# Gate steps placed behind the sums of squares, weight copies each released at its own slot, and a reordered end of attention, in a fused attention and top-capacity MoE kernel

## The chip, the core and the metric

The kernel runs on one core of one Trainium2 chip. The metric is the device time of one execution in microseconds. Before the change it is 424.39 us, the median of 3 runs (422.96 to 424.91).

## What is computed

Attention with RMS-normed q and k (8 batches, 12 heads, 448 tokens, head size 64, all float32), then a mixture of experts on its output (3584 tokens of 768 features, 8 experts, hidden size 1024, at most 80 tokens for each expert).

```
q_n, k_n = rmsnorm(q, g_q), rmsnorm(k, g_k)
attn = softmax(q_n @ k_n.T / sqrt(64))          # the 1e-9 in the sum left aside
x = (attn @ v) as 3584 x 768
logits = x @ w_gate;  expert = argmax(logits);  gate_w = softmax(logits)[expert]
for each expert e:
    tok = tokens of e; if more than 80: the 80 with the largest gate_w
    out[tok] = gate_w[tok] * (relu(x[tok] @ w1[e]) @ w2[e])      # all other rows are 0
```

## The kernel before

**Tiling.** A batch has 12 heads, handled as 3 groups of 4 heads, so there are 24 groups. A group has 7 rows of work: `score` makes a [128, 2, 448] tile of transposed scores (L359) and its exponential (`at`, L362), `av` adds it into `po` (L376), `presum` adds it on VectorE into `sm`, the sums of the softmax (L392, L394).

**Slots.** The order on every engine is written out by hand. The loop at L791 walks over slots; slot s scores rows 2s and 2s+1 and finishes rows 2s-2 and 2s-1, so 3.5 slots are a group, 10.5 a batch and 84 (NS) the whole of attention. Other work hangs on slots in tables: `begins` (ahead of the scores), `pre`, `mid` (behind the presums), `ahead` and `end` (behind `av`). Engines run their own queues in that order, so a step that waits holds up all that stands behind it on its engine.

**Preparing a group.** A group's q and k are loaded by SyncE (L242). ScalarE squares them (L270), VectorE sums the squares (`ms`, L278), ScalarE makes 1/rms from them (`rs`, L289, L290), VectorE refines it (L291 to L293) and scales q and k (`qn`, L306), TensorE transposes (L314), ScalarE copies out of PSUM (`qkT`, L347, L349). The tiles of q and k have four buffers, that is two groups.

**PSUM.** Scores, half of the transposes and the gate's scratch share one tag, `sc`, with two buffers: the next score must wait until ScalarE has emptied the tile two places earlier.

**The gate of a batch** follows 5 to 9 slots behind the start of its third group (b0): `zl` (L411) and `gate1` bring logits and softmax sums together, `gate1v` (L439) divides them, `gate2` (L465) finds maximum and one-hot, `gate2x` takes the exponential and copies the one-hot (L481, L483, ScalarE), `gate2b` the gate's weight `gw` (L489, L491), `gate2p` splits it into bf16 parts on GpSimd (L518 to L521, L512). `merge` then puts the batch's best 80 tokens of each expert into a running list: `row`, `vbeat`, `vtied`, `vahead`, `counts`, `vput`, `place`, `turn`.

**Weights.** The first three experts' weights are fetched straight into SBUF (`fetch_held`, L669), the other five are cast into a bf16 scratch in DRAM by 20 copies from GpSimd's queue (`stage_w`, L201 to L205) and read from there later by SyncE (`fetch_late`).

**The end.** L828 to L935 do the last batch's gate and merge step by step, with filler matmuls (`busy`) that keep TensorE running. Then each expert gathers its rows (L925), transposes them (`xpose`) and runs two matmuls (L973, L992). Weights of the sixth expert (NW0+2) are fetched at L873 and L964, those of the last two when the first two experts are done.

Of the kernel before, what the change touches and what calls it, by code (L numbers as in the profile page):

```python
# [10 lines left out]
F32 = mybir.dt.float32  # L11
# [10 lines left out]
def kernel(  # L22
# [13 lines left out]
    nc = tc.nc  # L36
# [161 lines left out]
    def staged(e, i):  # L198
        return wb_dram[e - NW0, i].rearrange("(c p f) -> p c f", p=128, c=(DC, FC)[i])

    def stage_w(e, i, half):  # L201
        src = (moe_w1, moe_w2)[i][e].rearrange("(c p) f -> p c f", p=128)
        c = src.shape[1] // 2
        nc.gpsimd.dma_start(out=staged(e, i)[:, half * c:half * c + c],
                            in_=src[:, half * c:half * c + c])  # L205
# [27 lines left out]
    with av_stack:  # L233
# [290 lines left out]
        def merge(b):  # L524
# [76 lines left out]
            def vput():  # L601
# [8 lines left out]
                    m["put"][:], iota[:, :].unsqueeze(1).to_broadcast([128, NT, CAP]),  # L610
                    rank[:].unsqueeze(2).to_broadcast([128, NT, CAP]), op=ALU.is_equal)
                m["keep"] = tpool.tile([CAP, E, CAP], BF16, tag="keep", name="keep")
                nc.vector.tensor_tensor(
# [15 lines left out]
            def turn():  # L629
                ps = scratch(BF16)  # L630
                for r in range(2):
# [4 lines left out]
            return [[row, lambda: vbeat((0, 1))], [experts, lambda: vbeat((2, 3)), vtied],  # L636
                    [own, vahead], [counts, vput], [place], [turn]]

# [56 lines left out]
        def at_slot(where, s, f, *a):  # L695
            where.setdefault(s, []).append((f, a))

        ahead = {}

# [17 lines left out]
        for g in range(NG):  # L717
# [3 lines left out]
            if g:  # L721
                for a in range(2):
                    at_slot(mid, b0 - 7 + a if g > 1 else -1, square, g, a)
                    at_slot(end, b0 - 7 + a if g > 1 else -1, squares, g, a)
                at_slot(mid, b0 - 5 if g > 1 else 0, rstd, g)
                for a in range(2):
                    at_slot(mid, b0 - 5 + a if g > 1 else 0, normalise, g, a)
            if g:
# [6 lines left out]
        for b in range(B):  # L735
# [12 lines left out]
            at_slot(end, b0 + 6, gate1t, b)  # L748
            at_slot(mid, b0 + 7, gate1v, b)
            at_slot(mid, b0 + 7, gate2, b)  # L750
            at_slot(mid, b0 + 8, gate2i, b)
            at_slot(end, b0 + 8, gate2x, b)
            at_slot(pre, b0 + 9, gate2b, b)
            at_slot(pre, b0 + 9, gate2p, b)
            for t, fs in enumerate(merge(b)):


                if b == B - 2 and t > 3:
                    at_slot(end, b0 + 12 + t, fs[0])
                    continue  # L760
                s = 15 + b % 2 if b < B - 2 else 13
                (first if t else lambda *a: at_slot(end, *a))(
                    b0 + (10, 10, 12, s, 18 + b % 2, 20 + b % 2)[t], fs[0])
                for n, f in enumerate(fs[1:]):
                    at_slot(end, b0 + (10, 11, 12, s)[t], f)
        at_slot(begins, 0, load_wgs)
# [10 lines left out]
        for e in range(E):  # L777
            for i in range(2):
                s = 9 + 23 * (2 * e + i) // 5
                if e < NW0:  # L780
                    at_slot(mid, s, fetch_held, e, i)
                    continue
                for half in range(2):
                    at_slot(begins, s + 2 * half, stage_w, e, i, half)

# [5 lines left out]
        for s in range(-10, NS + 6):  # L791
# [16 lines left out]
            for r in A2:  # L808
                if r % RD < RD - 1 or r == A2[-1]:
                    av(r)  # L810
            for f, a in ahead.pop(s, []) + end.pop(s, []):
                f(*a)
        assert not ahead
        assert not begins and not pre and not mid and not end
# [36 lines left out]
    for j in range(NT):  # L851
        nc.tensor.matmul(psa[:, 1, j * CAP:(j + 1) * CAP], eqT[:, j * 128:(j + 1) * 128],
                         listT[:3 * E, :], start=True, stop=True)
    busy(4)
    gate2p(b)
    ahead = tpool.tile([128, NT, CAP], BF16, tag="ahead", name="ahead")
    nc.vector.tensor_tensor(
        ahead[:], psa[:, 1, :NT * CAP].rearrange("p (j c) -> p j c", c=CAP),
        gw.unsqueeze(2).to_broadcast([128, NT, CAP]), op=ALU.is_lt)
    R, back = psa[:, 0, :NT * E], psa[:CAP, 1, NT * CAP:NT * CAP + E]  # L860
    for i in range(NT):
# [8 lines left out]
        if i == 0:  # L870

            nc.vector.memset(w_tiles[NW0 + 2][0][0][:, 0, 0:2], 0.0)
            fetch_late(NW0 + 2, (0, ))  # L873
            for j in range(NT):
# [8 lines left out]
                         listn[:CAP, :5])  # L883
    for j in range(NT):
        nc.vector.scalar_tensor_tensor(
            tied[:, j], row[:, j * 128:(j + 1) * 128], gw[:, j:j + 1], tri[:, :],
            op0=ALU.is_equal, op1=ALU.mult)
    for j in range(NT):
# [10 lines left out]
                            rank[:].unsqueeze(2).to_broadcast([128, NT, CAP]), op=ALU.is_equal)  # L899
    psc = scps.tile([128, 2, 512], F32, tag="sc", name="psc")  # L900

    moves = [(identb[:CAP, :CAP], left)] + [(put[:, j, :], m["info"][:, j]) for j in range(NT)]
# [38 lines left out]
    def xpose(e):  # L941
        xg = xgs[e]
        xn = mpool.tile([CAP, DM], BF16, tag="xn", name="xn")
        for i in range(NQ):
# [4 lines left out]
                xg[:, DM + 4 * i:DM + 4 * i + 4].rearrange("p (u hh) -> p u hh", hh=2)  # L949
                .unsqueeze(3).to_broadcast([CAP, 2, 2, D]))  # L950
        pxt = mps.tile([128, DC, CAP], BF16, tag="pxt", name="pxt", bufs=1)
        for c in range(DC):
# [9 lines left out]

    nc.vector.memset(w_tiles[NW0 + 2][1][0][:, 0, 0:2], 0.0)
    fetch_late(NW0 + 2, (1, ))  # L964
    busy(2)
# [78 lines left out]
```

## Time and profile before

| | us |
|---|---|
| median of 3 runs | 424.39 |
| profiled execution | 423.0 |
| its span in the trace | 421.3 |
| attention, first score to the last `po` matmul | 15.6 to 356.1 |
| last gate and gather, until the first expert matmul | 356.1 to 377.3 |
| eight experts | 377.3 to 415 |

TensorE is busy for 399.1 us of the span, VectorE for 357.5, ScalarE for 314.9, GpSimd for 73.5. Attention is 340 us of it, and there all three large engines have little air; the end is a chain of short steps on one engine after the other. TensorE's granted clock is full throughout, but for the store of the last rows.

### The profile page before, as it was taken

The page shows a single profiled execution, that of the slowest core. Times are in us where ns is not written, and L with a number is a line of the kernel's source. Part 1 is how long each engine was busy: PE and PEld are TensorE (multiplying, and loading weights), DVE is VectorE, ACT ScalarE, POOL GpSimd, SP SyncE. Part 2 cuts the span into 40 slices and gives each one's busy share as a digit, 9 for nine tenths or more (in the row PEclk, how much of TensorE's full clock was granted, in tenths as well). Part 3 has the DMA queues.
Part 4 walks back from the last instruction along what each step waited for, and adds up shares of the span by engine and source line. Part 5 has one row for each costly group of instructions (what it writes and reads, how often), then busy time and mean ns, then how long its engine had stood idle before and what let it go on. Part 6 is the DMA issues. An engine that isn't in the chain of part 4 may idle for free.

```text
span 421.3 us, 12543 instructions
## 1 busy us (share of the span) xinstructions
PE 399.1 (95%) x5289; PEld 194.9 (46%) x5289; DVE 357.5 (85%) x641; ACT 314.9 (75%) x479; POOL 73.5 (17%) x118
## 2 busy tenths in 40 slices
PE   6799999999989999999899999999999999889993
PEld 6334444444444445444444444443444443448882
DVE  5699889998999999989999999989999779735550
ACT  5898979997889799979798799878997784202120
POOL 2000001301040205100420024001500050134321
PEclk9999999999999999999999999999999999999999
DMA  7355599999959999999799969999799298869981
GB/s 261 123 149 140 152 224 317 282 254 268 287 166 206 326 230 274 242 237 320 234 236 233 338 172 195 232 286 338 170 237 312 59 358 211 270 213 339 342 301 47
DMA packets 75983, 100.91 MB, mean 240 GB/s; under 512 B 8344, under 2 KB 65176, under 8 KB 75928
## 3 DMA queue, kind: packets, MB, share of 16 engines
q1 hardware_dynamic: 59856, 70.53, 52.2%
q0 software_dynamic: 15776, 29.13, 36.1%
q8 instruction: 41, 0.67, 0.6%
q10 hardware_dynamic: 296, 0.46, 0.4%
q14 instruction: 14, 0.11, 0.1%
HBM read 101.11 MB, written 39.89 MB: 335 GB/s over the span
## 4 chain that ended last, share of the span: by engine, by line
PE 69%; DMA 12%; DVE 10%; ACT 5%; issue 2%; SPq 0%; POOLq 0%; DVEq 0%; ACTq 0%
PE ps L359 26%; PE po L376 26%; DMA w_sb<-wb_scratch 5%; PE zl L411 4%; DMA qk<-in_k_dram 4%; PE tp L314 3%; PE xp L314 3%; DVE ms L278 2%; DVE sm L394 2%; DMA xr_scratch<-xb 2%; PE py L992 1%; DVE qn L306 1%; PE ph L973 1%; ACT qkT L349 1%; DMA xg<-xr_scratch,idxG 1%
## 5 line engine op out<-in xcount | busy, mean ns | idle before, releaser
L359 PE MATMUL ps<-qkT 64*64 64x448 f32 x1344 | 147.9, 548 | 7.6 <-ACT qkT L349 3.2
L362 ACT ACTIVATE at<-ps 128x896 f32<-128x896 f32 x168 | 146.4, 931 | 2.5 <-PE ps L359 1.6
L376 PE MATMUL po<-at,vt 64*64 64x448 f32 x1344 | 142.4, 537 | 0.1
L394 DVE TENSOR_TENSOR sm<-sm,at 128x896 f32<-128x896 f32 x120 | 132.0, 1100 | 2.9
L376 PEld LDWEIGHTS po<-at,vt 64*64 64x64 f32 x1344 | 50.0, 133 | 74.9 <-issue 64.3
L359 PEld LDWEIGHTS ps<-qkT 64*64 64x64 f32 x1344 | 43.1, 132 | 73.2 <-issue 23.5
L278 DVE TENSOR_REDUCE ms<-sq 128x14 f32<-128x896 f32 (+1 forms) x50 | 51.9, 1044 | 6.6 <-ACT sq L270 6.4
L306 DVE TENSOR_TENSOR qn<-qk,rs 128x896 f32<-128x896 f32 (+1 forms) x50 | 52.5, 1052 | 1.9
L270 ACT ACTIVATE sq<-qk 128x896 f32<-128x896 f32 (+1 forms) x50 | 46.3, 929 | 2.8 <-DMA qk<-in_q_dram 2.8
L518 POOL CAST pt<-gw 128x4 bf16<-128x4 f32 x8 | 6.9, 866 | 201.9 <-DVE gw L491 201.9
L977 ACT ACTIVATE h_sb<-ph 128x320 bf16<-128x320 f32 x16 | 7.0, 437 | 39.8 <-PE ph L973 39.8
L654 ACT COPY xb<-xp 128x1024 f32<-128x1024 f32 x24 | 24.3, 1011 | 9.7 <-PE xp L314 9.6
L314 PEld LDWEIGHTS tp<-ident,qn 64*128 64x128 f32 x672 | 23.4, 139 | 11.1 <-issue 5.3
L314 PE MATMUL tp<-ident,qn 64*128 64x64 f32 x672 | 26.9, 226 | 0.0
L383 ACT COPY us<-po 128x896 f32<-128x896 f32 (+1 forms) x24 | 21.4, 893 | 6.2 <-PE po L376 6.2
L392 DVE TENSOR_TENSOR sm<-at 128x896 f32<-128x896 f32 x24 | 25.9, 1081 | 0.0
L347 ACT ACTIVATE qkT<-tp,gqk 128x896 f32<-128x896 f32 x23 | 23.5, 1023 | 0.0
L349 ACT COPY qkT<-tp 128x896 f32<-128x896 f32 x24 | 21.9, 913 | 1.3 <-PE tp L314 1.2
L992 PE MATMUL py<-w_sb,h_sb 128*80 128x384 bf16 (+1 forms) x136 | 22.2, 317 | 0.6 <-DMA w_sb<-wb_scratch 0.6
L996 DVE TENSOR_SCALAR yo<-py,gwT 80x384 f32<-80x384 f32 (+1 forms) x16 | 9.5, 600 | 14.9 <-PE py L992 14.7
L411 PE MATMUL zl<-us,wgs 64*32 64x448 f32 x192 | 21.0, 540 | 0.0
L411 PE MATMUL zl<-sm,zsel 64*32 64x448 f32 x192 | 20.5, 540 | 0.0
(170 smaller groups left out, 412.0 us busy)
## 6 DMA issues: line engine op xcount, KB each, us to landing
wb_scratch<-in_moe_w_dram POOLq DMA_DIRECT2D x20, 768.0 KB, 14.9
w_sb<-wb_scratch SPq DMA_DIRECT2D x9, 1536.0 KB, 8.1
vt<-in_v_dram SPq DMA_DIRECT2D x24, 448.0 KB, 6.3
out_dram<-zeros SPq DMA_DIRECT2D x28, 384.0 KB, 8.2
qk<-in_q_dram SPq DMA_DIRECT2D x23, 448.0 KB, 5.0
qk<-in_k_dram SPq DMA_DIRECT2D x23, 448.0 KB, 6.6
xr_scratch<-xb SPq DMA_DIRECT2D x48, 192.0 KB, 10.2
w_sb<-in_moe_w_dram POOLq DMA_DIRECT2D x6, 1536.0 KB, 15.7
```

What stands on the lines that cost most here:

```text
L270: nc.scalar.activation(st[g]["sq%d" % a][:, lo:hi], st[g]["qk"][a][:, lo:hi], AF.Square)
L278: nc.vector.reduce_sum(out=st[g]["ms"][:, a, lo:hi], in_=st[g]["sq%d" % a][:, lo:hi], axis=AX.X)
L306: nc.vector.tensor_mul(qn[:].rearrange("p (x hh) d -> p hh x d", hh=2)[:, h0:h1], qk[:, lo:hi].rearrange("p (hh x) d -> p hh x d", x=NX), ...
L314: nc.tensor.transpose(o, w, one[p, p], tile_position=(p.start, 0))
L349: nc.scalar.copy(T[:], tp[:, :, :S])
L359: nc.tensor.matmul(ps[u * 64:u * 64 + 64, hh, :S], T1[d, u, x * 64:(x + 1) * 64], T0[d, u, :], start=True, stop=True)
L362: nc.scalar.activation(at[:], ps[:, :, :S], AF.Exp)
L376: nc.tensor.matmul(po[u][hh * D:(hh + 1) * D, u, :S], vt[p, hh * NX + x, :], at[p, hh, :], start=(x == 0), stop=(x == RD - 1))
L392: nc.vector.tensor_add(s["sm"][:], s["at0"][:], s["at1"][:])
L394: nc.vector.tensor_add(s["sm"][:], s["sm"][:], s["at%d" % x][:])
L411: nc.tensor.matmul(t[32 * c:32 * c + 32, r, :S], w, x, start=(i == 0), stop=(i == NQ - 1))
L992: nc.tensor.matmul(py[:, :c1 - c0], h_sb[:, fc, :], chunk(e, 1, fc)[:, c0:c1], start=(fc == 0), stop=(fc == FC - 1))
```

## The change

Six things move.

- **Gate on VectorE and ScalarE.** `gate1v` goes from the middle of its slot to the end, `gate2` from the middle of slot b0+7 to the end of b0+8, and `gate2x`, `gate2b` and `gate2p` to the end of b0+9. So the next group's sums of squares stand ahead of them. The first `normalise` of a batch's first group goes behind the slot's end (`after`), and `vtied` one slot later.
- **Copies.** Each of the 20 copies of weights gets a marker: VectorE sets one element at the copy's slot, GpSimd copies it onto itself and then issues the copy, so that GpSimd can't run ahead of VectorE. The slots are evenly spaced, 2.25 apart from slot 31 to 73; the six direct fetches are at slots 4 to 26 (9 to 32 before).
- **One-hots later.** For the batch before the last, `vput` stands behind the last presums and `keep` at the slot's end.
- **Ties.** In the last merge ScalarE makes the differences gw - row in bf16, and one VectorE instruction over 512 elements makes the ties from them; before, four instructions over 128 each compared and masked.
- **`back`** has its own PSUM tile.
- **Late fetches.** The sixth expert's first weights are fetched right behind `gate2p`, its second ones behind the first expert's first scaled piece.

```diff
+    mark = cpool.tile([1, 4 * (E - NW0)], BF16, name="mark")
     def stage_w(e, i, half):
+        n = 4 * (e - NW0) + 2 * i + half
+        nc.vector.memset(mark[:, n:n + 1], 0.0)
+        nc.gpsimd.tensor_copy(mark[:, n:n + 1], mark[:, n:n + 1])
         src = (moe_w1, moe_w2)[i][e].rearrange("(c p) f -> p c f", p=128)
...
-                    [own, vahead], [counts, vput], [place], [turn]]
+                    [own, vahead], [counts, vput, vkeep], [place], [turn]]
...
-                    at_slot(mid, b0 - 5 + a if g > 1 else 0, normalise, g, a)
+                    s = b0 - 5 + a if g > 1 else 0
+                    at_slot(after if not a and g % NQ == 0 and g > NQ else mid, s, normalise, g, a)
...
-            at_slot(mid, b0 + 7, gate1v, b)
-            at_slot(mid, b0 + 7, gate2, b)
-            at_slot(mid, b0 + 8, gate2i, b)
-            at_slot(end, b0 + 8, gate2x, b)
-            at_slot(pre, b0 + 9, gate2b, b)
-            at_slot(pre, b0 + 9, gate2p, b)
+            at_slot(end, b0 + 7, gate1v, b)
+            at_slot(end, b0 + 8, gate2, b)
+            at_slot(end, b0 + 8, gate2i, b)
+            at_slot(end, b0 + 9, gate2x, b)
+            at_slot(end, b0 + 9, gate2b, b)
+            at_slot(end, b0 + 9, gate2p, b)
...
-                    at_slot(end, b0 + (10, 11, 12, s)[t], f)
+                    if b == B - 2 and t == 3:
+                        at_slot((mid, end)[n], NS, f)
+                    else:
+                        at_slot(end, b0 + (10, 11 + n, 12, s)[t], f)
...
-                s = 9 + 23 * (2 * e + i) // 5
+                n = 2 * e + i
                 if e < NW0:
-                    at_slot(mid, s, fetch_held, e, i)
+                    at_slot(mid, 4 + 9 * n // 2, fetch_held, e, i)
                     continue
                 for half in range(2):
-                    at_slot(begins, s + 2 * half, stage_w, e, i, half)
+                    at_slot(mid, 4 + 9 * (2 * n + half) // 4, stage_w, e, i, half)
...
-            for f, a in ahead.pop(s, []) + end.pop(s, []):
+            for f, a in ahead.pop(s, []) + end.pop(s, []) + after.pop(s, []):
...
     gate2p(b)
+    nc.vector.memset(w_tiles[NW0 + 2][0][0][:, 0, 0:2], 0.0)
+    fetch_late(NW0 + 2, (0, ))
...
-    R, back = psa[:, 0, :NT * E], psa[:CAP, 1, NT * CAP:NT * CAP + E]
+    psc = scps.tile([128, 2, 512], F32, tag="sc", name="psc")
+    R, back = psa[:, 0, :NT * E], psc[:CAP, 1, 64:64 + E]
+    for j in range(NT):
+        nc.scalar.activation(tied[:, j], row[:, j * 128:(j + 1) * 128], AF.Identity,
+                             scale=-1.0, bias=gw[:, j:j + 1])
...
-            nc.vector.memset(w_tiles[NW0 + 2][0][0][:, 0, 0:2], 0.0)
-            fetch_late(NW0 + 2, (0, ))
...
-    for j in range(NT):
-        nc.vector.scalar_tensor_tensor(
-            tied[:, j], row[:, j * 128:(j + 1) * 128], gw[:, j:j + 1], tri[:, :],
-            op0=ALU.is_equal, op1=ALU.mult)
+    nc.vector.scalar_tensor_tensor(
+        tied[:], tied[:], 0.0, tri[:, :].unsqueeze(1).to_broadcast([128, NT, 128]),
+        op0=ALU.is_equal, op1=ALU.mult)
...
+            if e == 0 and i == 0:
+                nc.vector.memset(w_tiles[NW0 + 2][1][0][:, 0, 0:2], 0.0)
+                fetch_late(NW0 + 2, (1, ))
```

**Place 1, VectorE at the gate of batch 3** (of 0 to 7; sm are the presums, rz and lx are `gate1v`, lg to eq are `gate2`, ms the sums of squares of a later group), before the change:

```order
L394 TENSOR_TENSOR sm<-sm,at 128x896 x2
L445 RECIPROCAL rz<-zs 128x12x2 x2
L453 TENSOR_TENSOR lx<-zs,rz 128x12x8 x4
L468 TENSOR_REDUCE lg<-lx 128x32
L471 TENSOR_REDUCE lmax<-lg 128x4
L474 TENSOR_TENSOR lex<-lg,lmax 128x32
L476 TENSOR_TENSOR eq<-lg,lmax 128x32
L477 MEMSET eq 64x8
L278 TENSOR_REDUCE ms<-sq 128x14
L392 TENSOR_TENSOR sm<-at 128x896
L278 TENSOR_REDUCE ms<-sq 128x14
L489 TENSOR_REDUCE lsum<-lex 128x4
```

The same place after the change:

```order
L205 MEMSET mark 1x1
L283 TENSOR_REDUCE ms<-sq 128x14
L450 RECIPROCAL rz<-zs 128x12x2 x2
L458 TENSOR_TENSOR lx<-zs,rz 128x12x8 x4
L397 TENSOR_TENSOR sm<-at 128x896
L283 TENSOR_REDUCE ms<-sq 128x14
L473 TENSOR_REDUCE lg<-lx 128x32
L476 TENSOR_REDUCE lmax<-lg 128x4
L479 TENSOR_TENSOR lex<-lg,lmax 128x32
L481 TENSOR_TENSOR eq<-lg,lmax 128x32
L482 MEMSET eq 64x8
L399 TENSOR_TENSOR sm<-sm,at 128x896 x2
```

All of `gate2` stands behind the second ms now, and `gate1v` behind the first; lsum comes after two more presums.

**Place 2, ScalarE at the same point** (at are the exponentials of scores, rs the 1/rms of a later group, qkT the copies of the transposes of the next one, lex and eqb `gate2x`), before the change:

```order
L627 CAST listn<-mp 80x40
L481 ACTIVATE lex<-lex 128x32
L483 CAST eqb<-eq 128x288
L362 ACTIVATE at<-ps 128x896 x2
L289 ACTIVATE rs<-ms,eps 128x28
L290 ACTIVATE rs<-rs 128x28
L349 COPY qkT<-tp 128x896
L347 ACTIVATE qkT<-tp,gqk 128x896
L362 ACTIVATE at<-ps 128x896 x2
```

The same place after the change:

```order
L634 CAST listn<-mp 80x40
L367 ACTIVATE at<-ps 128x896 x2
L294 ACTIVATE rs<-ms,eps 128x28
L295 ACTIVATE rs<-rs 128x28
L354 COPY qkT<-tp 128x896
L352 ACTIVATE qkT<-tp,gqk 128x896
L486 ACTIVATE lex<-lex 128x32
L488 CAST eqb<-eq 128x288
L367 ACTIVATE at<-ps 128x896 x2
```

The two short instructions of `gate2x` moved from ahead of one pair of exponentials to ahead of the next.

**Place 3, VectorE at the end of attention** (rnk to put are `vput`, us is half of the copy of the last `po`, zsb the last batch's `gate1`), before the change:

```order
L603 TENSOR_TENSOR rnk<-back,eq 128x32
L605 TENSOR_REDUCE rank<-rnk 128x4
L606 SCALAR_TENSOR_TENSOR rank<-rank,cnt 128x4
L609 TENSOR_TENSOR put<-iota,rank 128x320
L613 TENSOR_TENSOR keep<-iota,move 80x640
L394 TENSOR_TENSOR sm<-sm,at 128x896 x2
L385 COPY us<-po 128x448
L418 TENSOR_REDUCE zsb<-zl 128x256
```

The same place after the change:

```order
L399 TENSOR_TENSOR sm<-sm,at 128x896 x4
L608 TENSOR_TENSOR rnk<-back,eq 128x32
L610 TENSOR_REDUCE rank<-rnk 128x4
L611 SCALAR_TENSOR_TENSOR rank<-rank,cnt 128x4
L614 TENSOR_TENSOR put<-iota,rank 128x320
L390 COPY us<-po 128x448
L620 TENSOR_TENSOR keep<-iota,move 80x640
L423 TENSOR_REDUCE zsb<-zl 128x256
```

The last presums pass all of `vput` and keep, and us passes keep.

## Rows read from the trace of the kernel before

**Rows 1.** Page, first part: busy us (share of the span) x instructions, by engine

```profile
PE 399.1 (95%) x5289; PEld 194.9 (46%) x5289; DVE 357.5 (85%) x641; ACT 314.9 (75%) x479; POOL 73.5 (17%) x118
```

**Rows 2.** Waits of PE, 20 to 352 us: total us, times, longest us

```profile
PE ps L359 <- ACT qkT L349: 3.2, 3, 1.2
PE ps L359 <- ACT row L543: 1.3, 3, 0.4
```

**Rows 3.** Timeline, 200 to 222 us: start, duration, engine, line, [idle before <-releaser]

```profile
200.56 0.86 DVE L468 TENSOR_REDUCE lg<-lx 128x32 f32<-128x384 f32 x1
...
201.91 0.23 ACT L481 ACTIVATE lex<-lex 128x32 f32<-128x32 f32 x1 [0.97 <-DVE lex L474]
...
202.13 1.09 DVE L278 TENSOR_REDUCE ms<-sq 128x14 f32<-128x896 f32 x1
...
202.13 0.43 ACT L483 CAST eqb<-eq 128x288 bf16<-128x288 f32 x1
...
204.13 1.08 DVE L278 TENSOR_REDUCE ms<-sq 128x14 f32<-128x896 f32 x1
...
205.25 0.32 ACT L289 ACTIVATE rs<-ms,eps 128x28 f32<-128x28 f32 x1 [1.05 <-DVE ms L278]
...
206.67 0.98 PE L359 MATMUL ps<-qkT 64*64 64x448 f32 x8 [1.23 <-ACT qkT L349]
...
211.63 0.98 PE L359 MATMUL ps<-qkT 64*64 64x448 f32 x8 [0.44 <-ACT row L543]
```

**Rows 4.** Timeline, 200 to 222 us: GpSimd, and VectorE beside it

```profile
207.74 0.20 POOL L520 CAST pt<-left 128x4 bf16<-128x4 f32 x1
...
209.29 2.47 DVE L394 TENSOR_TENSOR sm<-sm,at 128x896 f32<-128x896 f32 x2
...
213.67 2.21 DVE L394 TENSOR_TENSOR sm<-sm,at 128x896 f32<-128x896 f32 x2
```

**Rows 5.** The tile qk: who waited (us, times), landing

```profile
  DMA qk<-in_q_dram: 2.8, 3
...
DMA to landing us min/median/max: 3.1/5.3/17.8
```

**Rows 6.** Timeline, 352 to 372 us, the end of attention and the gate

```profile
354.14 0.81 DVE L613 TENSOR_TENSOR keep<-iota,move 80x640 bf16<-80x640 f32 x1
...
354.88 2.21 DVE L394 TENSOR_TENSOR sm<-sm,at 128x896 f32<-128x896 f32 x2
...
357.13 0.13 PEld L411 LDWEIGHTS zl<-sm,zsel 64*32 64x32 f32 x2 [0.29 <-DVE sm L394]
...
357.67 0.10 PEld L411 LDWEIGHTS zl<-us,wgs 64*32 64x32 f32 x1 [0.40 <-DVE us L385]
...
364.20 0.59 ACT L849 COPY row<-psb 128x512 f32<-128x512 f32 x1
```

**Rows 7.** Timeline, 367.5 to 377.4 us, the last merge and the first transpose

```profile
367.19 0.81 PE L822 MATMUL hot<-tri,identb 128*128 128x512 bf16 x3
...
367.37 0.22 DVE L879 TENSOR_SCALAR stay<-psa,rowF 80x8 bf16<-80x8 f32 x1 [0.35 <-PE psa L868]
...
367.72 1.13 DVE L885 SCALAR_TENSOR_TENSOR tied<-row,gw,tri 128x128 bf16<-128x128 f32 x4
...
369.12 0.19 DVE L893 TENSOR_TENSOR place<-psa,eq 128x32 f32<-128x32 f32 x1 [0.27 <-PE psa L891]
...
377.19 0.06 DVE L963 MEMSET w_sb<- 128x1 uint32 x1
```

**Rows 8.** Groups of instructions: busy us, mean ns | idle before

```profile
L559 DVE TENSOR_TENSOR tied<-row,gw 128x512 bf16<-128x512 f32 x7 | 4.8, 687 | 0.0
...
L561 DVE TENSOR_TENSOR tied<-tied,tri 128x512 bf16<-128x512 bf16 x7 | 3.0, 425 | 0.3
```

**Rows 9.** Chain of waits, 350 to 421.3 us: start, us

```profile
389.00 22.25 DMA w_sb<-wb_scratch
```

**Rows 10.** Timeline, 372 to 422 us, the last expert

```profile
411.74 2.61 PEld L992 LDWEIGHTS <-h_sb 128*80 128x80 bf16 x24 [0.75 <-ACT h_sb L977]
```

More of the change, by code (lines that the diff above doesn't have):

```diff
@@ L611, in vput, with vkeep @@
                     rank[:].unsqueeze(2).to_broadcast([128, NT, CAP]), op=ALU.is_equal)
+            def vkeep():
                 m["keep"] = tpool.tile([CAP, E, CAP], BF16, tag="keep", name="keep")
@@ L696, in at_slot @@
             where.setdefault(s, []).append((f, a))
-        ahead = {}
+        ahead, after = {}, {}
         def first(s, f, *a):
@@ L810 @@
                     av(r)
-            for f, a in ahead.pop(s, []) + end.pop(s, []):
+            for f, a in ahead.pop(s, []) + end.pop(s, []) + after.pop(s, []):
                 f(*a)
-        assert not ahead
+        assert not ahead and not after
         assert not begins and not pre and not mid and not end
@@ L899 @@
                             rank[:].unsqueeze(2).to_broadcast([128, NT, CAP]), op=ALU.is_equal)
-    psc = scps.tile([128, 2, 512], F32, tag="sc", name="psc")
     moves = [(identb[:CAP, :CAP], left)] + [(put[:, j, :], m["info"][:, j]) for j in range(NT)]
@@ L961 @@
     xpose(0)
-    nc.vector.memset(w_tiles[NW0 + 2][1][0][:, 0, 0:2], 0.0)
-    fetch_late(NW0 + 2, (1, ))
     busy(2)
```

## The prediction

> **What bounds the kernel now.** I read the busy shares first, then TensorE's waits, then the timeline at the place of those waits, then the chain through the end. TensorE is busy for 95% of the span, VectorE for 85% [rows 1]; in attention both are near full, so only two kinds of time can come back: TensorE's waits, and the chain of short steps after the last score. Between 20 and 352 us TensorE waits for two things only: three times for ScalarE's copy of transposes (3.2 us) and three times for ScalarE's copy of the row of gate weights (1.3 us) [rows 2]. They come in pairs, in batches 1, 3 and 5, so a pair costs 1.23 + 0.44 = 1.67 us [rows 3] and all three 4.5.
>
> How a pair arises is seen in batch 3 [rows 3]. VectorE works through the gate from 199.4 us; gate2 alone takes from 200.56 to 202.13, and only then come the sums of squares, the second of which ends at 204.13 + 1.08 = 205.21. ScalarE's L289 needs them and began at 205.25 after 1.05 us of idling. Behind it in ScalarE's queue stand the copies of the transposes, whose PSUM tile TensorE's next score needs. So VectorE's gate reaches TensorE through ScalarE's order, not directly.
>
> **The gate moved: -2.1 us.** In the new order gate2's 202.13 - 200.56 = 1.57 us stands behind the second sum, which then ends at 203.64, before ScalarE is free at 205.25 - 1.05 = 204.20. The whole 1.05 us of idling goes, and of TensorE's first wait 1.23 - 1.05 = 0.18 is left. But lex and eqb, 0.23 + 0.43 = 0.66 us [rows 3], now stand between the copies and the next exponentials. Before, they lay ahead of an earlier pair, where ScalarE waited 0.97 us for them. From that point on ScalarE is only 1.05 - 0.66 = 0.39 us ahead, and the row copy that ends the second wait is in its queue. So a batch gives back between 0.39 (ScalarE decides to the end) and 1.67 (TensorE does). The wait of 0.44 for the row says that ScalarE ends the stretch, so I stay near the lower end: 0.7 a batch, 2.1 for three, with ends 1.2 and 4.5. In batches 0, 2 and 4 lex and eqb also move ahead of other exponentials. Rows 2 shows no wait of TensorE there, so I cost it at nothing; if that cover is missing it is 3 x 0.66 = 2.0 us lost, and the worst for this part is 2.0 - 1.2 = 0.8 us slower. What is late next is the gate's weight gw, now two presums and a refinement later on VectorE; the row's transposes wait for it, and about nothing remains of its air.
>
> **The copies: 0.** VectorE gets 20 more settings of 0.06 us (as one of the same kind takes, the last row of [rows 7]), 1.2 us in all, and GpSimd 20 copies of one element, 0.2 us each when undisturbed [rows 4]. Behind a waiting marker in GpSimd's queue stand the weight copy and gate2p, whose results are first needed several slots later. The number of copies and their bytes stay; only their times move. At best ScalarE's three waits for q, 2.8 us [rows 5], go; I count none of it, since TensorE's waits don't name it. The bad side is the third rival. The six direct fetches come some 5 slots earlier and wait for nothing.
>
> One thing speaks against the markers. A pair of presums took 2.47 us beside GpSimd's instructions and 2.21 in quiet [rows 4], 0.26 more; if each marker holds VectorE up for its own 0.2 us, that is 4 us of VectorE's time over 42 slots, 0.1 a slot. I cost that at nothing, because TensorE waits for no VectorE instruction in rows 2. [...]
>
> **The end of attention: -0.6 us.** keep took 0.81 us ahead of the last presums, which ran from 354.88 [rows 6], and TensorE's zl then waited 0.29 us for the presums and 0.40 for VectorE's half of us. Now keep stands behind us, which can start 0.81 us earlier, near the end of the last po matmul at 356.1. The 0.29 goes wholly, and most of the 0.40: 0.6, with ends 0.3 and 0.69. keep itself is needed only by a later place, and VectorE idles for zl meanwhile.
>
> **The ties: -0.6 us.** stay waited 0.35 us for the last counts, since back lay in the same tile [rows 7]; with a tile of its own it starts when VectorE is free. The ties took 1.13 us as four instructions. One over 512 elements isn't in the trace in this form; the nearest are 425 ns with bf16 inputs and 687 with a float32 one [rows 8]. I take 0.69, the dearer, since I don't know that this operation gains from bf16. Ties then end at 367.72 - 0.35 + 0.69 = 368.06 and not 368.85: 0.79 earlier. TensorE's fillers run to 367.19 + 0.81 = 368.00, so they no longer hide anything, and three pairs of small matmuls that ran in VectorE's shadow (place began 369.12 - 368.85 = 0.27 behind the last tie) now follow the ties; between 0 and 0.6 us, I take 0.15, as they are a few columns each. That leaves 0.64, with ends 0.19 and 0.35 + 1.13 - 0.43 = 1.05. ScalarE's four differences start behind its copy of row, 364.20 + 0.59 [rows 6], and take between 4 x 0.23 and 4 x 0.43 by the two short instructions of rows 3, so they are ready by 366.5 at the latest, before 367.37.
>
> [...]
>
> **The late fetches: 0.** Their settings of 0.06 us only change place. The transfers start earlier: the one moved behind the first scaled piece by about the rest of xpose. It matters because the last expert's second weights landed at 389.00 + 22.25 = 411.25 [rows 9], and TensorE took them at 411.74, held up by h_sb at that point [rows 10]. So there was 0.49 us of air. If the end gains 1.24 us and the transfers nothing, 0.75 us of it are lost again; I expect the fetches to move with the rest and count nothing.
>
> **Sum.** -2.1 - 0.6 - 0.64 = -3.3 us. Against the profiled execution (423.0, its span 421.3 and 1.7 around it) that is 419.7. The median of the runs is 1.4 above that execution; the same difference from 424.39 gives **421.0**. The ends of all parts together, without the third rival: -4.5 - 0.69 - 1.05 - 2.8 = -9.0 and +0.8 - 0.3 - 0.19 + 0.75 = +1.1.
>
> **Rivals.** First, all of TensorE's 4.5 us come back: -4.5 - 1.24 = -5.7, 418.7. For it: the first wait is the larger and hangs on the sums alone. Against it: the 0.66 us put into ScalarE's queue. Second, attention gives nothing: the stretch is as long as ScalarE's and VectorE's work in it, and lex, eqb and the later gw take back what the earlier sums gave. Then only the end is left, -1.24, 423.1. For it: both engines have no idle time from 205.3 to 211.6 but fractions. Against it: the idling of 0.97 and 1.05 us which surely goes. Third, slower: q and k come too late. Their buffers are freed four slots ahead of the squares, at 340 / 84 = 4.05 us a slot 16.2 us; landings had a median of 5.3 and a longest of 17.8, and three late ones cost 2.8 us, 0.93 each [rows 5]. From landings over 16.2 us on it decides. If copies that are always under way do that to half of the 12 groups loaded between slots 31 and 73, it costs 5.6 us, and with -3.3 the time is 426.7. Against it: bursts behind gate2p loaded the queues as much already, and the typical landing has a threefold margin.
>
> Fourth, all of the markers' 4 us reach TensorE, and the sum is +0.7: 425.1. For it: the 0.26 us beside GpSimd. Against it: VectorE has 15% of the span free, and TensorE waits for it nowhere in attention.
>
> **Chances.** My forecast 0.46, the first rival 0.20, the second 0.23, the third 0.08, the fourth 0.03. The measurement can't tell less than about 0.5% (2.1 us) from no change. Faster by more, below 422.3: most of the forecast, all of the first rival and a little of the second, 0.63. Within it: the rest of the forecast, nearly all of the second rival and the fourth, 0.29. Slower: the third, 0.08. The range runs from a little past the first rival, 417.8, to a little past the second, 424.0.
>
> **What would show it.** In the profile after: L289's successor no longer waits for the second sum in batches 1, 3 and 5, and TensorE's wait for the transposes' copy is below 0.3 us there while that for the row stays at some tenths; zl no longer waits for sm or us; stay follows the last comparison at once, and one instruction of 0.4 to 0.7 us makes the ties; the last weights land before h_sb is ready. I am wrong if TensorE waits as long as before at the odd gates, if new waits come up at the even ones, for gw or for ScalarE's exponentials, or if ScalarE's waits for q and k grow beyond 3 us.

## The result, and the profile after

The changed kernel takes **418.44 us**, median of 6 runs (417.47 to 419.24); the kernel before 424.34, median of 6 (422.83 to 424.91). The ratio is 0.988, with a 95% interval of 0.985 to 0.990. In a later session the same pair gave 418.91 and 423.53, 0.990 (0.987 to 0.994). By the two ratios 5.2 and 4.1 us are gone, where I had forecast 3.3.

The profiled execution took 417.47 us, its span 415.7, against 423.0 and 421.3. Busy us and share by engine, first part of the page after (it answers to [rows 1]; PE is TensorE, PEld its weight loads, DVE VectorE, ACT ScalarE, POOL GpSimd):

```profile
PE 397.6 (96%) x5289; PEld 194.2 (47%) x5289; DVE 354.6 (85%) x658; ACT 315.9 (76%) x483; POOL 81.3 (20%) x138
```

TensorE's waits between 20 and 352 us, after (total, times, longest), beside [rows 2]:

```profile
PE ps L364 <- ACT row L548: 1.3, 3, 0.4
PE mp L319 <- ACT at L367: 0.7, 3, 0.2
```

The 3.2 us for the transposes' copy are gone, the row's 1.3 us have stayed, and a small wait for ScalarE's exponentials has come. How long a batch takes is read between the starts of zl. These are from the chain of waits (start, us), of before:

```profile
98.17 2.50 PE zl L411 x48
144.57 2.50 PE zl L411 x48
185.60 2.50 PE zl L411 x48
232.00 2.50 PE zl L411 x48
```

and of after:

```profile
98.42 2.50 PE zl L416 x48
143.66 2.50 PE zl L416 x48
184.69 2.50 PE zl L416 x48
229.92 2.50 PE zl L416 x48
```

A stretch that holds an odd gate took 144.57 - 98.17 = 46.40 and takes 143.66 - 98.42 = 45.24; one with an even gate takes 41.03 in both. So an odd batch gives 1.16 us, and batches 2 and 4 neither pay nor gain (batch 0 pays 0.10).

The rows of the same place as [rows 3], a batch's gate (batch 3) after, from the timeline:

```profile
200.31 1.73 ACT L367 ACTIVATE at<-ps 128x896 f32<-128x896 f32 x2 [0.29 <-PE ps L364]
...
201.54 1.08 DVE L283 TENSOR_REDUCE ms<-sq 128x14 f32<-128x896 f32 x1
...
202.54 0.87 DVE L473 TENSOR_REDUCE lg<-lx 128x32 f32<-128x384 f32 x1
202.66 0.32 ACT L294 ACTIVATE rs<-ms,eps 128x28 f32<-128x28 f32 x1 [0.62 <-DVE ms L283]
...
204.89 0.23 ACT L486 ACTIVATE lex<-lex 128x32 f32<-128x32 f32 x1
205.01 0.43 ACT L488 CAST eqb<-eq 128x288 bf16<-128x288 f32 x1
...
205.33 0.93 ACT L367 ACTIVATE at<-ps 128x896 f32<-128x896 f32 x1
```

The sums now stand ahead of lg; lex and eqb follow the copies and wait for nothing. The exponentials that had stood behind lex and its 0.97 us of idling start at 200.31, right when their score is done.

The end of attention, after (timeline; beside [rows 6]; the tile zl ends with the product that began at 353.48, 1.28 us long):

```profile
353.06 0.62 DVE L390 COPY us<-po 128x448 f32<-128x448 f32 x1
...
353.59 0.81 DVE L620 TENSOR_TENSOR keep<-iota,move 80x640 bf16<-80x640 f32 x1
...
354.79 1.15 DVE L423 TENSOR_REDUCE zsb<-zl 128x256 f32<-128x512 f32 x2 [0.39 <-PE zl L416]
```

keep stands behind us, and VectorE then waits for zl, no longer zl for VectorE. The last merge, after (timeline; beside [rows 7]):

```profile
360.87 1.28 ACT L876 ACTIVATE tied<-row,gw 128x128 bf16<-128x128 f32 x4
...
362.97 0.22 DVE L894 TENSOR_SCALAR stay<-psc,rowF 80x8 bf16<-80x8 f32 x1
...
363.31 0.68 DVE L899 SCALAR_TENSOR_TENSOR tied<-tied,tri 128x512 bf16<-128x512 bf16 x1
```

stay waits for nothing, and one instruction of 0.68 us makes the ties. Adding up, from the two profiled executions (before, after, difference):

| stretch | before | after | difference |
|---|---|---|---|
| start to the first zl | 57.73 | 57.88 | +0.15 |
| first zl to the seventh | 261.71 | 258.31 | -3.40 |
| seventh zl to the end of the last | 39.27 | 38.57 | -0.70 |
| end of the last zl to the first expert's product | 18.59 | 17.82 | -0.77 |
| first expert's product to the end | 44.00 | 43.12 | -0.88 |
| span | 421.3 | 415.7 | -5.6 |

Of the 0.88 us at the experts, 0.81 arise where the last expert begins its second products. TensorE there, of before:

```profile
409.25 1.88 PE L973 MATMUL ph<-xgT,w_sb 128*128 128x80 bf16 x48
411.77 1.39 PE L992 MATMUL py<-w_sb,h_sb 128*80 128x384 bf16 x11 [0.64 <-DMA w_sb<-wb_scratch]
```

and of after:

```profile
404.48 1.88 PE L986 MATMUL ph<-xgT,w_sb 128*128 128x80 bf16 x48
406.19 2.79 PE L1005 MATMUL py<-w_sb,h_sb 128*80 128x384 bf16 x24
```

2.52 us between the two starts before, 1.71 after. The second line of before says what my reading of [rows 9, 10] had missed: TensorE had waited 0.64 us for the transfer itself.

### The profile page after: what moved, and what is told of

It is laid out like the page before. It is cut to its first block, busy times and chain, and to the rows that moved or that the text cites. A ratio compares the mean times of both kernels' runs of the same rounds, so it can differ in the third digit from the quotient of the medians.

```text
span 415.7 us, 12591 instructions
## 1 busy us (share of the span) xinstructions
PE 397.6 (96%) x5289; PEld 194.2 (47%) x5289; DVE 354.6 (85%) x658; ACT 315.9 (76%) x483; POOL 81.3 (20%) x138
## 4 chain that ended last, share of the span: by engine, by line
PE 87%; ACT 5%; DVE 3%; issue 2%; DMA 2%; POOLq 0%
PE ps L364 32%; PE po L381 29%; PE zl L416 5%; PE py L1005 4%; PE tp L319 4%; PE xp L319 3%; PE ph L986 3%; ACT at L367 1%; ACT zsb L426 1%; DMA xg<-xr_scratch,idxG 1%; PE mp L594 1%; DMA qk<-in_q_dram 1%; ACT zo L428 1%; ACT xb L661 1%; PE mp L319 1%
## 5 line engine op out<-in xcount | busy, mean ns | idle before, releaser
L399 DVE TENSOR_TENSOR sm<-sm,at 128x896 f32<-128x896 f32 x120 | 130.5, 1087 | 3.1
L206 POOL COPY mark<-mark 1x1 bf16<-1x1 bf16 x20 | 7.5, 376 | 138.2 <-DVE mark L205 138.2
## 6 DMA issues: line engine op xcount, KB each, us to landing
wb_scratch<-in_moe_w_dram POOLq DMA_DIRECT2D x20, 768.0 KB, 10.3
w_sb<-wb_scratch SPq DMA_DIRECT2D x9, 1536.0 KB, 10.3
```

The lines of the kernel that those rows point to most:

```text
L399: nc.vector.tensor_add(s["sm"][:], s["sm"][:], s["at%d" % x][:])
```

## The experiments

Each part of the change was put into the kernel before by itself, then single costs were added or moved in the kernel after. Taken together the parts are the kernel after.

**The gate's order alone.**

```
-at_slot(mid, b0 + 7, gate1v, b)   ...   +at_slot(end, b0 + 7, gate1v, b)
-at_slot(mid, b0 + 7, gate2, b)    ...   +at_slot(end, b0 + 8, gate2, b)
(and gate2i, gate2x, gate2b, gate2p, the first normalise, vtied as in the change)
```

> The kernel before with the order of the gate's steps alone (gate steps behind the sums of squares, the normalise of each odd batch's first group last in its slot, the ties one slot later). Theory: TensorE's wait for the copies of the transposes was VectorE's gate reaching it through ScalarE's queue, and this order alone takes it out whole: each odd batch, measured from one start of zl to the same of the next batch, shortens from 46.40 to 45.2 us, even batches stay within 0.1 of 41.03 and 40.44, the wait for the row stays at 0.44 three times, and the time falls by 3.4 to 3.7 us, to about 420.8. Rival (the copies' new spacing did it): the odd batches keep 46.4 and the time stays within 0.5 us of before. Rival (my forecast: ScalarE's exponentials behind lex and eqb take most of it back): 45.7 a batch and 2.1 us in all.

Measured: 420.33 us, median of 10, against 423.45 of 31 runs of before on the same chip, ratio 0.992 (0.990 to 0.994), so -3.5 us with bounds of -2.6 and -4.4. TensorE's waits between 20 and 352 us:

```profile
PE ps L359 <- ACT row L543: 1.3, 3, 0.4
PE mp L314 <- ACT at L362: 0.7, 3, 0.2
```

They are those of the kernel after, with one more of 0.3 us. The odd batches take 45.23 us, so the first theory holds and both rivals fall: the order of the gate is worth 3 x 1.16 = 3.5 us, not the spacing of the copies, and not my 2.1. One thing the theory had not: batch 4 took 41.58 us, 0.54 more than in the kernel after, so that the six stretches together gained 2.9 us in this profile and not 3.4. ScalarE waited there for a late q, and TensorE then for ScalarE (the 0.3 us):

```profile
242.08 0.95 ACT L270 ACTIVATE sq<-qk 128x896 f32<-128x896 f32 x1 [0.43 <-DMA qk<-in_q_dram]
```

**The copies in their new slots alone.**

```
+nc.vector.memset(mark[:, n:n + 1], 0.0); nc.gpsimd.tensor_copy(mark[:, n:n + 1], ...)
-at_slot(begins, 9 + 23 * (2 * e + i) // 5 + 2 * half, stage_w, e, i, half)
+at_slot(mid, 4 + 9 * (2 * n + half) // 4, stage_w, e, i, half)
(and the six direct fetches at their new slots)
```

> The kernel before with the weights' copies alone in their new slots, each behind its marker. Theory: nothing in attention changes; the odd batches keep 46.40 us and the even ones 41.03, and the time stays within 0.5 us of before; VectorE's waits for the markers cost no TensorE time. Rival 1: the evenly spread copies let q and k land sooner, ScalarE's waits for them fall from 2.8 to about 1.4 us and some tenths of each batch come back, 1 us or more in all. Rival 2: each marker holds up VectorE and through it TensorE, and the time grows by 0.5 us or more.

Measured: 423.70 us, ratio 1.001 (0.999 to 1.003). The chain of waits has zl at

```profile
98.24 2.50 PE zl L416 x48
144.61 2.50 PE zl L416 x48
185.64 2.50 PE zl L416 x48
```

46.37 and 41.03 us. ScalarE's waits for q fell from 2.8 to 1.6 us and nothing of it reached TensorE, whose wait for the transposes' copy even read 3.7 us. By themselves markers and spacing are worth nothing, either way. But they do what they were made for, as the tile qk shows:

```profile
DMA to landing us min/median/max: 3.2/5.5/9.7
```

The longest landing of q or k is 9.7 us here and 9.1 to 10.3 in the eight other profiles with the new slots; with the old ones it is 17.5 to 18.2 in all five. Behind the first 24 us ScalarE waits for q once or twice in each of these five profiles and never in the nine. In the order of before such a wait cost TensorE nothing; in the new order one of 0.43 us went with the 0.54 us that batch 4 lost in the experiment above. What the spacing is worth together with the gate's order stays open: that one profile shows half a microsecond.

**The last weights' fetches alone.** The two settings and `fetch_late` calls of the sixth expert moved as in the change.

> The kernel before with the last weights' two fetches issued earlier, and nothing else. Theory: in the kernel before TensorE stood 0.8 us at the last expert's second products for the last weights' transfer, not for ScalarE's h_sb, so the time from that expert's first product to its first second product falls from 2.52 to 1.7 us and the time by 0.8 us; everything ahead of the experts keeps its place to 0.2 us. Rival (my forecast: h_sb is what TensorE waits for): the 2.5 us stay and the time stays within 0.3 us of before, and what the kernel after shows there came from its other parts.

Measured: 423.49 us, ratio 1.001 (0.997 to 1.004). The 1.72 us between the last expert's two starts are there as the theory said, but so they are in every other profile of this study, also in those with the fetches at their old place, as in the next experiment's:

```profile
409.03 1.88 PE L974 MATMUL ph<-xgT,w_sb 128*128 128x80 bf16 x48
410.75 2.46 PE L993 MATMUL py<-w_sb,h_sb 128*80 128x384 bf16 x20
```

So the theory was wrong: TensorE's 0.64 us for the transfer belonged to the one execution that was profiled before. From issue to landing the last transfer took 22.6 us in it and 20.2 to 22.0 in the four other profiles with the fetches at their old place, where it landed 0.2 to 2.0 us ahead of its products. The 0.88 us of the table are not shown to be the change's; they are nearly all that one late transfer.

**The ties and the tile of its own alone.**

```
+nc.scalar.activation(tied[:, j], row[...], AF.Identity, scale=-1.0, bias=gw[:, j:j + 1])
-nc.vector.scalar_tensor_tensor(tied[:, j], row[...], gw[:, j:j + 1], tri, ...)   (four)
+nc.vector.scalar_tensor_tensor(tied, tied, 0.0, tri, ...)                        (one)
```

> The kernel before with the ties from ScalarE's differences and the PSUM tile of its own for back, and nothing else. Theory: from the end of zl to the experts' first product 18.59 us become about 17.8, as in the kernel after; but the last weights' transfer is issued a few tenths earlier at most, so TensorE's wait for it grows by what it no longer takes as cover and the time falls by at most 0.4 us. Rival (my forecast: the transfers move with the rest): the whole 0.6 to 0.8 us reach the end.

Measured: 422.91 us, ratio 0.999 (0.997 to 1.002), a difference too small for the runs to tell. In the trace the last zl ends at 357.31 + 1.97 = 359.28 and the experts begin at 377.07, 17.79 us later: 0.80 less than before. They then take 43.23 us, so in this trace all of it reached the end; the part of my expectation that set 0.4 us as a limit fell with the wait of the experiment above.

**keep behind the last presums alone.**

```
-at_slot(end, b0 + 13, vput + vkeep)   (b == B - 2)
+at_slot(mid, NS, vput); at_slot(end, NS, vkeep)
```

> The kernel before with put and keep of the last batch but one put behind the last presums, and nothing else. Theory: attention to the start of the last zl (319.4 us) keeps its times to 0.2 us; there the second-to-last stretch shortens as in the kernel after: from the seventh zl's start to the end of the last zl 39.28 us become about 38.6, the gain 0.7 us. Rival: the presums aren't what zl waits for and under 0.2 us come back.

Measured: 421.36 us in one run, too few to tell by the time. From the seventh zl (319.23) to the end of the last, in the chain of waits of this kernel,

```profile
356.54 1.28 PE zl L411 x16
```

are 357.82 - 319.23 = 38.59 us, 0.68 less. The parts add to 3.5 + 0.7 + 0.8 = 5.0 us, where the whole measured 5.2 and 4.1.

**eqb copied twice, in the kernel after.**

```
+for _ in range(2):
     nc.scalar.copy(gst[b]["eqb"], gst[b]["eq"][:]...)
```

> The kernel after with ScalarE's copy eqb done twice in each batch but the last, 0.32 to 0.43 us more of ScalarE's queue at the place where the gate order put it. Theory (ScalarE sets the odd batches' length from the copies of the transposes to the row, so what came back is ScalarE's idling at the gate's old place, 0.97 us, which my forecast left out): each odd batch grows from 45.24 to 45.55 to 45.65 us, even ones stay at 41.03 and 40.5 within 0.1, the wait for the exponentials (three times 0.2 us) or for the row (three times 0.4) grows by as much, and the kernel loses about 1.1 us. Rival (TensorE sets the length, ScalarE has air): the odd batches stay within 0.1 of 45.24.

Measured: one run, 421.48 us. Waits of TensorE between 20 and 352 us, then zl in the chain of waits:

```profile
PE mp L319 <- ACT at L367: 1.8, 3, 0.6
PE ps L364 <- ACT row L549: 1.3, 3, 0.4
```

```profile
98.86 2.50 PE zl L416 x48
144.56 2.50 PE zl L416 x48
185.90 2.50 PE zl L416 x48
```

An odd batch takes 45.70 us, 0.46 more, and the wait for the exponentials has grown by about as much (1.1 us for three). ScalarE has no air there and does decide the odd batches. Batches 2 and 4, 41.34, grew by 0.31, where I had expected no change (batch 0 by 0.09): there too what is added to ScalarE's queue lengthens the batch, though no row names it as a wait.

**The first normalise back at its old place, in the kernel after** (`after` taken out, `mid` for all).

> The kernel after with the normalise of each odd batch's first group back at its former place in the middle of its slot. Theory: the sums of squares and ScalarE's root are what the gate's steps held up, so this step's place gives little: odd batches stay within 0.3 us of 45.24. Rival: at its former place this 1.08 us instruction of VectorE stands ahead of the gate's comparison and exponentials' sum, gw and the row come as much later, and the odd batches lengthen by 0.6 to 1.1 us.

The edit moves it in every batch from the third on, not in the odd ones alone. Measured: 419.68 us in one run, odd batches 45.31 us, 0.08 more. A wait of 1.6 us (three times, 0.6 at most) for gw came up, the one I had named as a danger of the new order, and it hardly lengthened them. Batch 0 paid more: 40.93 us and not 40.54, with a wait of TensorE of 0.3 us for ScalarE's own. First to seventh zl is 258.93 us, 0.6 more than after, so this step's place is worth that much in one profile.

**The row's copy ahead of xb's, and eqb on GpSimd, in the kernel after.**

```
 (t == 0: row)  -at_slot(end, b0 + 10, row)   +first(b0 + 10, row)   (behind experts)
```

> The kernel after with the row of gate weights turned and copied behind the experts' one-hots and ahead of xout's transposes and their 1.0 us copy, in every batch's merge. Theory: the wait of TensorE's score for the row's copy (three times 0.44 us) goes, as ScalarE reaches that copy 1.0 us sooner; xb's copy then lies in front of the next exponentials as both copies did before, so a part may come back as a wait for these; the odd batches become 44.8 to 45.0 us and the time falls by 0.7 to 1.3 us. Rival (ScalarE's total decides the stretch, the order of its copies doesn't): odd batches stay at 45.2 and the wait only changes its name.

Measured: 419.00 us, median of 4, ratio 0.986 (0.981 to 0.991). Waits of TensorE between 20 and 352 us:

```profile
PE mp L319 <- ACT listT L642: 0.8, 3, 0.3
PE mp L319 <- ACT at L367: 0.7, 3, 0.2
```

The row's wait is gone, the odd batches take 44.66 us, 0.58 less; but another wait came, and batches 2 and 4 pay 0.35 each (41.38). From the first zl to the seventh it is 257.26 us, 1.05 less than 258.31.

```
-nc.scalar.copy(gst[b]["eqb"], ...)   +nc.gpsimd.tensor_copy(eqb, ...)
```

> The kernel after with the copy eqb on GpSimd, directly behind the comparison that makes its input, in place of ScalarE. Theory (ScalarE sets the odd batches' length): the 0.32 to 0.43 us leave ScalarE's queue, each odd batch shortens by 0.2 to 0.4 us (the wait for the exponentials of 0.2 us goes, that for the row shrinks), the time falls by 0.6 to 1.2 us. Rival: eqb comes so late from GpSimd that the transposes of the one-hots wait for it, or GpSimd holds VectorE's presums up, and nothing or less than nothing is won.

Measured: 419.45 us, median of 4, ratio 0.988 (0.983 to 0.992). Odd batches 44.89, 0.35 less, batches 2 and 4 41.19 and 41.14, up to 0.16 more. The copy takes 1.28 us on GpSimd (mean of 7) and TensorE doesn't wait for it. The exponentials behind its old place in batch 2:

```profile
164.55 1.73 ACT L367 ACTIVATE at<-ps 128x896 f32<-128x896 f32 x2 [0.37 <-PE ps L364]
```

They start 164.55 - 144.91 = 19.64 us behind zl, as in the kernel after, and now wait for TensorE's score. So at an even gate ScalarE and TensorE arrive together: more work for ScalarE lengthens the batch, less of it gives nothing.

**The kernel after again, with fillers, and with the odd batches' copies moved.**

> The kernel after, unchanged, as the measure for the next two beside it. Theory: its parts add to 3.5 us from the gate's order, 0.7 from put and keep and 0.75 from the ties, so it stands 4.9 us below before, at about 418.5; what a run shows beyond that is TensorE's granted clock, at half its level for up to 6 us in the first 20 us of some executions and for about 4 us at the first expert's products in others. Rival: something in the whole is worth more than its parts, and it stands 6 us or more below.

Measured: 418.91 us, median of 6, ratio 0.990 (0.987 to 0.994), 4.1 us below before (2.8 to 5.5). The sum of the parts lies inside, the rival's 6 us outside.

```
+(fill, 3) behind the first transposes;   -busy(18)   +busy(22)
```

> The kernel after with three more filling products of TensorE between the first and the second transposes at the start, and four more while the first expert's rows are gathered; they fill TensorE's idle stretches of 2.3 and 1.2 us and write to tiles that nobody reads. Theory (the granted clock falls behind these idle stretches and costs 1.3 us at the start and 1.5 at the experts in some executions): no profile shows a clock under 0.9 outside the ends, the first zl starts at 57.5 to 57.9 us, the experts take 43.1 to 43.2, and the median falls by 0.5 to 2 us against the kernel after. Rival (the clock falls whatever fills these gaps, or the fillers stand in the way): the median is the same or worse.

Measured: 419.91 us, ratio 0.991 (0.988 to 0.994): nothing won. The granted clock (third number from the end; the second number is TensorE's busy time) fell at the start all the same, with the three products in the idle stretch; windows of after_fill:

```profile
12.00:16.00 4.00, 2.97 (x20) 0.88 (x24) 2.33 (x3) 3.71 (x5) 0.00 (x0) 0.67 0.50 189
16.00:20.00 4.00, 4.00 (x28) 1.27 (x24) 3.24 (x6) 3.50 (x7) 0.00 (x0) 0.50 0.14 18
```

So the theory failed at the start: the first zl came at 59.83 us, 2 us late. At the experts the clock stayed up in this profile; whether the four products there did that stays open (below).

```
+at odd b:  nc.gpsimd.tensor_copy(eqb, ...);  first(b0 + 10, row)   (and the fillers)
```

> The kernel after with the same fillers, and in odd batches alone the copy eqb on GpSimd and the row's copy ahead of xb's. Theory: the odd batches lose both of TensorE's remaining waits there and come to 44.2 to 44.5 us, even ones keep 41.03 and 40.5, since nothing in them changes; with the fillers the time is 2.5 to 4 us below the kernel after. Rival (TensorE's own work decides by then, or the even batches pay as they did when all rows were moved, 0.35 us each): under 1 us beyond the fillers alone.

Measured: **416.85 us**, median of 6 (416.57 to 417.52), ratio 0.985 (0.982 to 0.988), 2.1 us below the kernel after on the same chip; the two intervals overlap at their ends (0.987 to 0.994 there). zl in the chain of waits, and all that TensorE still waits for between 20 and 352 us:

```profile
184.20 2.50 PE zl L416 x48
228.93 2.50 PE zl L416 x48
270.12 2.50 PE zl L416 x48
```

```profile
PE mp L319 <- DVE gw L496: 1.0, 3, 0.3
```

Odd batches take 44.73 us, 0.5 less, batches 2 and 4 41.19, 0.16 more, though nothing in them was changed: 1.2 us in all over the six stretches, between theory and rival. ScalarE in batch 4 shows who asks for the 0.16:

```profile
258.33 0.32 ACT L294 ACTIVATE rs<-ms,eps 128x28 f32<-128x28 f32 x1 [0.32 <-DVE ms L283]
```

The sum of squares it waits for begins 257.21 - 228.93 = 28.28 us behind zl, in the kernel after (batch 2) 171.32 - 143.66 = 27.66, and there L294 doesn't wait. VectorE, whose work in the odd batch got no shorter, comes out of it 0.6 us late; it is busy for 312.1 of the 332 us from 20 to 352. The other 0.9 us of the median no row explains; in this profile the granted clock was 1.00 at the start and at the experts, and over the span of the six runs it was 0.992 to 0.998, in those of the kernel after 0.988 to 0.994.

## Why the prediction was right, and where it wasn't

**The gate: the mechanism right, the size wrong.** 1.16 us a batch and not 0.7. The step that failed is "before ScalarE is free at 205.25 - 1.05 = 204.20. The whole 1.05 us of idling goes", and after it "only 1.05 - 0.66 = 0.39 us ahead". I charged lex and eqb at their new place and left ScalarE's free time at its old value, as if they, and the 0.97 us of idling in front of them, still stood at the old one. In fact ScalarE was free at 200.31 + 1.73 = 202.04. Measured from zl's start, its L289 (now L294) came 205.25 - 185.60 = 19.65 us later before and 202.66 - 184.69 = 17.97 after: 1.68 earlier, as the sums were the later of the two, by 0.62 us of idling. From there to the next exponentials, of before

```profile
207.41 1.72 ACT L362 ACTIVATE at<-ps 128x896 f32<-128x896 f32 x2
```

ScalarE took 207.41 - 205.25 = 2.16 us before and 205.33 - 202.66 = 2.67 after, 0.51 more for lex and eqb. 1.68 - 0.51 = 1.17 is the whole gain, and the doubled eqb shows that this sum is ScalarE's: what was added to its queue there came out as time. My choice of ScalarE as the engine that ends the stretch was right; its row's wait stayed at 0.44 as I had said. That L289's successor would no longer wait was wrong, for the same reason.

**The even batches: nothing, as forecast**, but not for the reason given. That TensorE shows no wait there did not mean air: the doubled eqb cost 0.31 in batches 2 and 4. They came out even since lex and eqb only changed place in ScalarE's queue: the exponentials behind their new place start 19.64 us behind zl in both kernels.

**gw as the next late thing:** right in that it is near. It appears as a wait of up to 0.6 us when the first normalise stands ahead of it, and in the last kernel.

**The copies: 0, right by themselves**, and both the third and the fourth rival wrong: ScalarE's waits for q shrank, from 2.8 to 1.4 us (the 1.4, and 1.5 of the 2.8, are one wait in the first 24 us, so late landings had cost 1.3 in two waits and not 2.8 in three), as the longest landing fell from 17.8 to 9.5 us; and the presums beside GpSimd became shorter, not longer. The pair of 2.47 us came six times before, each time 0.94 or 0.95 us behind the start of GpSimd's info (L512), which took 1.34 us; in the kernel after info takes 0.46 to 0.66 and no such pair is left. The longest presum was 1348 ns before and is 1094:

```profile
L399 DVE TENSOR_TENSOR sm<-sm,at x120: 1058/1091/1094, 22.6 to 350.9; 128x896 f32<-128x896 f32 x120
```

(duration in ns, min, median and max, of the tile sm, after). With the gate's order alone the longest is 1094 too, with the copies alone 1347, so it was the order that parted them and not the copies.

**The end of attention: 0.6 forecast, 0.68 and 0.70 measured.** Both waits of zl went wholly, the upper end of the term.

**The ties: 0.64 forecast, 0.80 and 0.77 measured.** stay's 0.35 went, and the instruction took 0.68 us, as the float32 row had suggested (0.69), and not the bf16 row's 0.43. The 0.15 that I took off for the small products behind the ties came:

```profile
364.42 0.19 DVE L907 TENSOR_TENSOR place<-psa,eq 128x32 f32<-128x32 f32 x1 [0.42 <-PE psa L905]
```

place begins 364.42 - 363.99 = 0.43 us behind the ties, before 0.27: 0.16 lost. What was too small is the first term: stay begins 0.37 us behind the start of the last comparison (362.60 to 362.97), before 0.81 (366.56 to 367.37), so 0.44 came back where the row named 0.35.

**The fetches: 0, right by luck.** I read 0.49 us of air from [rows 9, 10], but the products had waited for the transfer in that one execution. The weight load's row names h_sb, the product's row the transfer. Every other profile begins these products on h_sb's first half, 1.71 to 1.72 us behind the first products, so it was the transfer that decided. Neither the moved fetches nor the shorter end shows a gain or a loss there.

**The first rival** came out nearly at the measured time (418.7), but not as it was told: of TensorE's 4.5 us 3.2 came back and 0.7 came new, 2.5 in all, where attention gained 3.4. A wait of 1.23 us cost more than its own time: the two halves of the score that it parted took 0.98 us each, the unbroken score takes 1.74, and `av` behind them begins 20.37 us after zl and not 21.87, 1.50 sooner. Around the new wait of 0.22 us 0.33 are lost again. The rest is from the end. The sum of the terms by the runs is 3.5 + 0.7 + 0.8 = 5.0 where I had 3.3.

## What to carry to other kernels

When a step is moved on an engine that takes its steps in the written order, as ScalarE does at the gate here, move its old cost too: take its duration and the idling ahead of it (0.66 and 0.97 us for lex and eqb) out of the engine's clock at the old place, carry that time forward to the point that decides, and only then charge it at the new one. A TensorE without waits in the profile is no proof of air on the engine that feeds it; adding a known cost to that engine's queue tells (the doubled eqb cost 0.31 us in batches 2 and 4). The addition tells what more work costs; whether less work gains has to be tried by itself. A part that measures nothing alone, as the spaced copies, may still guard another part: look at the longest landing (9.7 us with the new slots, 17.8 before), not only at the median (5.5 and 5.3). A wait in a single profile, as the 0.64 us for the last weights, is worth a look at a second execution before a term of a sum is made of it.

## What was not expected of the hardware

**TensorE's granted clock falls in some executions and not in others, at two places.** At the start it fell to 0.50 in eight of the fourteen profiles, the kernel after among them, for up to 7 us (as shown above for after_fill); in six it stood at 1.00 all through. Where its mean over the first 24 us is 1.00 (six profiles) the first zl starts at 57.5 to 57.8 us, at 0.93 (four) at 57.7 to 58.3, at 0.86 (four) at 59.0 to 59.8. The last kernel and after_fill have the same code there, and stand at 1.00 and 0.86. The other place is the first expert's products, behind a stretch in which TensorE does little while the rows are gathered (here 1.49 us of 3). Windows of after_eqb2 and of after, three us ahead of the first expert's first product and three behind it:

```profile
372.06:375.06 3.00, 1.49 (x10) 0.51 (x9) 1.56 (x6) 0.00 (x0) 1.93 (x2) 0.99 0.74 191
375.06:378.06 3.00, 3.00 (x46) 2.99 (x46) 0.95 (x3) 0.44 (x1) 0.00 (x0) 0.50 0.99 316
```

```profile
369.58:372.58 3.00, 1.53 (x10) 0.51 (x9) 1.56 (x6) 0.00 (x0) 1.89 (x2) 1.00 0.71 183
372.58:375.58 3.00, 3.00 (x61) 2.72 (x61) 1.36 (x5) 0.88 (x2) 0.16 (x1) 1.00 1.01 305
```

The same instructions ahead, 1.49 and 1.53 us of 3, and once the clock is 0.50 behind it and once 1.00. It costs 1.5 us: the experts take 44.64 us in place of 43.12. Four profiles show it, all of them of variants of the kernel after without more fillers, of which two others (after itself, twice) do not; the two with fillers (2.16 and 2.39 us busy) and the six of the kernel before and its single parts do not either. The busy time of these three us does not tell them apart: before had 1.51 and kept its clock, after_eqbpool had 1.55 and lost it. That is too few to say whether the shorter end makes the fall likelier or the fillers prevent it. The two places together can move a run by over 3 us, and that is one reason why a part worth 0.8 us is seen in the trace's stretches and not in a median of 10 runs.
